# Half sums of 1024 elements, chunk scores in pairs, and q of the first two batches in rows of six tokens

## The chip, the cores and the metric

One core of one Trainium2 chip runs the whole program in one launch. The metric is the time of one execution on the device in microseconds (us), as the median of several runs. The core has TensorE (PE in the profile, PEld for its weight loads), VectorE (DVE), ScalarE (ACT), GpSimd (POOL) and SyncE (SP), which issues most of the DMA transfers.

## The reference

The first part is a retention layer written as a recurrence over 768 tokens, for 4 batches, 8 heads and 64 dimensions a head. The second part takes its output as x (768 tokens, 512 channels), adds a low-rank mixing of the tokens, and runs a two-layer MLP with 2048 hidden units.

```python
for t in range(S):
    state = gamma[None, :, None, None] * state + np.einsum('bhd,bhe->bhde', k[:, :, t], v[:, :, t])
    y[:, :, t] = scale * np.einsum('bhd,bhde->bhe', q[:, :, t], state)
...
x = np.ascontiguousarray(attn_out.transpose(0, 2, 1, 3)).reshape(B, S, H * D)
xt = x.transpose(0, 2, 1)
h = xt @ U @ V
u = x + h.transpose(0, 2, 1)
ch = np.maximum(u @ w_ch1, 0.0) @ w_ch2
return (u + ch).astype(np.float32)
```

U is 768 x 32, V is 32 x 768, w_ch1 is 512 x 2048, w_ch2 is 2048 x 512. All inputs and the output are 32-bit floats.

## The kernel before

The recurrence is computed in blocks: inside a block as a masked product of scores and v, between blocks through a state. Decay factors are multiplied into q, k and v beforehand. Everything that TensorE reads is bf16.

**The attention of batches 0 and 1** is worked by pairs of heads (`pair`, c = 0 to 3). One load per pair brings 2 heads of k, q or v (`load_pair`, 384 KB): a piece of the load is two tokens of one head, 512 bytes, and 768 pieces make the load. The rows are converted to bf16 (`kb`, `qb`, `vb`), TensorE turns k and q with a unit matrix (`turn`, L528), ScalarE copies the turned k to `kT`, and VectorE multiplies the turned q with a table of factors `gqt` and writes `qT` in the order of tokens (L544). Then come scores (64 of the array's rows each), a masked copy `a` (L567), the states `ns`, and `mix`, which gives two blocks of x.

**The attention of batches 2 and 3** is worked by chunks of 128 tokens and all 8 heads (`loads_chunk`, `chunk`, n = 0 to 5). Here the DMA queue of SyncE turns k and q (rows `kT<-kb`, `qT<-qb`). The scores of a chunk are 8 matmuls on 64 rows each into the two banks RR0, RR1; VectorE masks them in one operation of 1024 elements (L700); `mixes` adds state and block products in RR2; the result is copied to x.

**The mixing**: `proj` computes x with U in two steps, for tokens 0 to 511 and 512 to 767 (each matmul on 32 columns of the array), `expand` the product with V on 32 rows, which VectorE adds to x (L770), and u is turned for the MLP.

**The MLP** (`mlp`): for each of 16 blocks of hidden units, matmuls of uT with w1b for 512 tokens (part 0), then for the other 256 tokens (part 1), each followed by a ReLU to `gT`. The second layer is computed in the manner of Strassen and Winograd, with seven products in place of eight for each 256 tokens (r = 0, 1, 2). It needs sums and differences of halves of gT (`S1`, `S2`, `S4`, and one in the place of a quarter of gT) and of w2 (`T2`, `T3`, `T4`, and one in place). `sums` makes those of gT with four VectorE operations of 512 elements a call, four calls for part 0 and two for part 1 in each batch; `w2_sums` makes those of w2 once, four calls of four operations. The products of each r go to the banks M0, M1 and M2 in turn (`prod`), and are gathered by ScalarE (`s1`), GpSimd (`t12`, `t22`, `t21`: rows `t<-s,x`) and VectorE (`r5`, `r6`, and the outputs `oa`, `ob`: rows `r` and `o`). GpSimd's queue stores the outputs; for the last batch SyncE's does.

**What sets the order.** Nothing is scheduled by the compiler. Each step is handed to `Plan.add` with its cost by engine, the names that it reads and writes, and a wished time. `Plan.run` walks through the steps with these costs, takes at each point the step that can start first (by wished time among equals), and so fixes for each engine the order in which its instructions stand. On the chip every engine works through its own queue in that order and waits by semaphores for what it needs. The planner also has a model of the DMA queues (`Queues`; a load is priced by pieces, each 0.009 us and its size over 27,200 a us). Where TensorE would be free in the first 27 us, `fill` puts in matmuls of zeros (rows `M<-gT`). A VectorE sum that reads two tiles and a GpSimd operation planned behind it are tied in this order by `behind`. The weights are loaded by GpSimd's queue, which converts them to bf16 (`load_cast`); the loads of batch 1 wait by `gate`, a copy of one element on GpSimd, for the second, third and fourth block of w2.

Of the kernel before, what the change touches and what calls it, by code (L numbers as in the profile page):

```python
# [18 lines left out]
class Step:  # L19
# [181 lines left out]
def kernel(  # L201
# [12 lines left out]
    P = 128  # L214
# [249 lines left out]
    def load_pair(nm, b, c, at, hold=0.0, after=None, halves=False):  # L464

        t, key = new_in()
# [3 lines left out]
        src = {"k": k, "q": q, "v": v}[nm][b, ds(2 * c, 2)]  # L470
        for g in ([(0,), (1,)] if halves else [(0, 1)]):
# [4 lines left out]
                 P * n, 512, [(key, i) for i in g], at + 0.01 * g[0], hold,  # L476
# [3 lines left out]
    def pair(b, c, at, first, atq=0.0, atv=0.0):  # L480
# [47 lines left out]
        def turn(dst, src):  # L528
            def f(e):
                for b0 in range(NB):  # L530
                    for j in range(2):
                        tp(dst[:, ts(2 * b0 + j, P)], src[:, ds(384 * j + P * b0, P)])
            return f
        add({"PE": 0.34}, turn(Yb, kb), both2(kbk) + ["ident"], ["Y"], at + 0.6, F,
            slack=sl)
# [4 lines left out]
        add({"PE": 0.34}, turn(tq, qb), both2(qbk) + ["ident"], [tqk], atq + 0.9, F,  # L540
            slack=sl)
        qTv = qT.rearrange("x (b p j) -> x b j p", b=NB, j=2)
        tqv = tq[:, :S].rearrange("x (b j p) -> x b j p", b=NB, j=2)
        add({"D": 1.03}, lambda e: nc.vector.tensor_tensor(  # L544
            qTv, tqv, gqt[:, c].rearrange("x (b p j) -> x b j p", b=NB, j=2),
            op=ALU.mult), [tqk, ("gqt", c)], [qTk], atq + 1.2)
# [115 lines left out]
    def chunk(b, n, at):  # L662
        (kin, kk), (qin, qk), (vin, vk) = (gets.pop((nm, b, n)) for nm in "kqv")
# [33 lines left out]
        add({"PE": 0.24}, score, [kTk, qTk], ["RR0", "RR1"], at, ("rw", "rw"),  # L697
            slack=sl)
# [3 lines left out]
            RR[0].rearrange("p i (n t) -> p (i n) t", t=P),  # L702
            mask[:, None, :].to_broadcast([P, H, P]), op=ALU.mult),
            ["RR0", "RR1", "mask"], zz(ak), at + 0.3)
# [8 lines left out]
        def mixes(e):  # L713
            if n:
                prev = ns[:, ds(4 * ((n - 1) % 5), 4)]
                for c in range(NC):
                    mm(RR[1][:, 0, ts(c, P)], qT[:, ts(c, P)], prev[:, c], start=(c == 0))
            for c in range(NC):
                for i in range(2):
                    h = 2 * c + i  # L720
                    mm(RR[1][:, 0, ts(h, D)], av[:, i, c], vd[:, ts(h, D)],
# [3 lines left out]
        if n < NCK - 1:  # L725
# [7 lines left out]
            [qTk, *nsk, *zz(ak), *zz(vdk)], ["RR2"], at + 1.9, F, slack=sl)  # L733
        evac(xs[b % 2][:, n], RR[1][:, 0], DM, ["RR2"], xk(b, [n], ALLC), at + 2.4)


    def proj(b, at):
        sl = 0.3

        def f(js):  # L740
# [6 lines left out]
        add({"PE": 0.25}, f(range(4)), xk(b, range(4), ALLC) + ["Ub"], ["Y"], at,  # L747
            ("cn", "cn"), slack=sl)
        add({"PE": 0.13}, f(range(4, 6)), xk(b, range(4, 6), ALLC) + ["Ub"], ["Y"],
            at + 0.1, ("cn", "cn"), slack=sl)  # L750
        evac(pcs, Y[:, :P], P, ["Y"], ["pcs"], at + 0.3)

    def expand(b, j0, nj, at):
# [9 lines left out]
        for j in range(j0, j0 + nj, 2):  # L763
            for z in range(2):
# [7 lines left out]
                    kk + [("u", b % 2, i, z) for i in (j, j + 1)], at + 0.3)  # L772
# [41 lines left out]
    def next_m():  # L814
        mring[0] += 1
        return f"M{(mring[0] - 1) % 3}"

    def mlp(b, T, span, banks=()):
# [26 lines left out]
        for m in range(NM):  # L845
# [21 lines left out]
            relu(gT[:, m, :LO], bank, [bank], [("g", m, 0)], at + 0.9)  # L867
        yield
        for m in range(0, NM, 2):
# [13 lines left out]
            relu(gT[:, ds(m, 2), LO:], bank, [bank], [("g", m, 1), ("g", m + 1, 1)],  # L883
# [6 lines left out]
        def sums(part, m0, nm_, at):  # L890
# [5 lines left out]
            ek = [("g", 2 * m, part) for m in range(m0, m0 + nm_)]  # L896
            ok = [("g", 2 * m + 1, part) for m in range(m0, m0 + nm_)]
# [315 lines left out]
```

## Time and profile before

| | |
|---|---|
| median of 3 runs | 223.75 us (223.63 to 224.15) |
| profiled execution | 224.59 us, span 222.8 us |
| TensorE clock granted | 0.997 on the mean |
| instructions in the profile | 5876 |
| DMA | 35.22 MB in 85163 packets, mean 158 GB/s |
| VectorE, ScalarE, GpSimd busy | 65%, 50%, 39% of the span |

The times of the rows are those of the profiled execution. A row of a group gives the line of the code, the engine, the operation, what is written and read by the program's names, the shapes and the count, then busy time and the mean of one, then the idle time of the engine just before them and what ended it. The matmuls, copies and sums are recorded by helpers, so that many have the same line (L305 all matmuls, L302 all operations on two tiles); they are told apart by their names.

### The profile page before, as it was taken

Reading aid. Unit: us, or ns where it says so; the run is one execution under the profiler, and the core shown is the slowest. Engines: PE = TensorE matmul, PEld = TensorE weight load, DVE = VectorE, ACT = ScalarE, POOL = GpSimd, SP = SyncE. Lnnn points to the kernel's source line nnn. Section 1 sums busy time; section 2 is a strip of 40 time slices with the busy share of each in tenths; the row PEclk is TensorE's granted clock in tenths of the full one; section 3 lists DMA queues with packets and bytes.
Section 4 is the critical chain, followed back from the end, with each engine's and each line's share of the span. In section 5 each row is a group of like instructions: output and inputs, shape, how many; then the busy total and the mean of one; then the engine's idle time right before and its main releaser. Section 6 shows DMA issues by size and latency. Waiting matters only on the chain.

```text
span 222.8 us, 5876 instructions
## 1 busy us (share of the span) xinstructions
PE 211.8 (95%) x2391; PEld 152.4 (68%) x2405; DVE 143.9 (65%) x297; ACT 111.7 (50%) x214; POOL 87.0 (39%) x143
## 2 busy tenths in 40 slices
PE   7867999999999999999999999999999999999993
PEld 2556644488788885457887875458888854588882
DVE  4486717998897636798677856867858525345332
ACT  8856537679684335678621105686510036761000
POOL 4665900114768554311368453316134510003330
PEclk9999999999999999999999999999999999999998
DMA  5999999999599979897479989986105730000222
GB/s 167 301 291 224 157 195 206 233 289 297 140 222 212 154 205 182 218 170 142 96 158 190 222 195 202 195 187 123 26 0 143 181 106 3 0 0 3 94 97 94
DMA packets 85163, 35.22 MB, mean 158 GB/s; under 512 B 59920, under 2 KB 83216, under 8 KB 85136
## 3 DMA queue, kind: packets, MB, share of 16 engines
q1 hardware_dynamic: 78944, 25.93, 55.0%
q0 software_dynamic: 6192, 8.91, 19.3%
q8 instruction: 19, 0.31, 0.6%
q14 instruction: 8, 0.07, 0.1%
HBM read 27.75 MB, written 6.29 MB: 153 GB/s over the span
## 4 chain that ended last, share of the span: by engine, by line
PE 63%; DVE 16%; DMA 7%; POOL 5%; issue 4%; ACT 2%; SPq 1%; POOLq 0%; DVEq 0%
PE M L305 51%; PE RR L305 8%; DVE S L302 4%; DMA in<-in_v_dram 4%; DMA in<-in_k_dram 3%; PE Y L305 3%; DVE T L302 2%; POOL t L302 2%; DVE x L770 2%; ACT gT L836 1%; DVE gT L302 1%; SPq L342 1%; DVE o L945 1%; POOL out_dram L987 1%; DVE x L299 1%
## 5 line engine op out<-in xcount | busy, mean ns | idle before, releaser
L305 PE MATMUL M<-uT,w1b 128*128 128x256 bf16 (+1 forms) x489 | 85.7, 324 | 0.7 <-issue 0.3
L836 ACT ACTIVATE gT<-M 128x512 bf16<-128x512 f32 x88 | 51.9, 597 | 34.1 <-PE M L305 33.5
L305 PEld LDWEIGHTS <-w1b 128*128 128x128 bf16 x512 | 48.0, 98 | 29.6 <-issue 0.8
L305 PEld LDWEIGHTS <-gT 128*128 128x128 bf16 x409 | 39.3, 99 | 10.6 <-issue 3.7
L302 POOL TENSOR_TENSOR t<-s,x 128x256 f32<-128x256 f32 x36 | 23.1, 669 | 34.9 <-DVE S L302 21.8
L305 PEld LDWEIGHTS <-S 128*128 128x128 bf16 (+1 forms) x336 | 28.1, 97 | 4.4 <-issue 0.4
L305 PE MATMUL M<-w2b,gT 128*128 128x256 bf16 x192 | 26.7, 273 | 0.1
L305 PE MATMUL M<-w2b,S 128*128 128x256 bf16 x192 | 26.1, 273 | 0.3 <-DVE r L945 0.3
L305 PE MATMUL M<-T,gT 128*128 128x256 bf16 x192 | 25.1, 273 | 0.5 <-DVE r L945 0.4
L302 POOL TENSOR_TENSOR qb<-in,gqn 128x512 bf16<-128x512 f32 x12 | 12.5, 1044 | 27.9 <-DVE S L302 11.6
L302 DVE TENSOR_TENSOR S<-gT 128x512 bf16<-128x512 bf16 x24 | 11.6, 485 | 18.0 <-ACT gT L836 17.9
L945 DVE TENSOR_TENSOR r<-M,t 128x256 f32<-128x256 f32 x24 | 10.1, 421 | 12.6 <-POOL t L302 11.7
L297 ACT ACTIVATE s<-M 128x256 f32<-128x256 f32 x12 | 4.6, 385 | 26.7 <-PE M L305 26.7
L987 POOL DMA_DIRECT2D out_dram<-o x18 | 10.1, 563 | 19.3 <-DVE o L945 19.3
L770 DVE TENSOR_TENSOR x<-RR,x 128x512 bf16<-128x512 f32 x24 | 15.2, 683 | 2.1 <-PE RR L305 2.1
L297 ACT ACTIVATE kb<-in 128x512 bf16<-128x512 f32 (+1 forms) x18 | 10.0, 582 | 13.0 <-DMA in<-in_k_dram 12.9
L700 DVE TENSOR_TENSOR a<-RR,mask 128x1024 bf16<-128x1024 f32 x12 | 14.6, 1218 | 1.4 <-PE RR L305 1.2
L302 POOL TENSOR_TENSOR vb<-in,gkn 128x512 bf16<-128x512 f32 x12 | 12.5, 1045 | 6.8 <-DMA in<-in_v_dram 3.0
L945 DVE TENSOR_TENSOR o<-M,r 128x256 f32<-128x256 f32 x24 | 10.1, 423 | 6.4 <-PE M L305 6.1
L305 PE MATMUL M<-T,S 128*128 128x256 bf16 x96 | 12.6, 273 | 0.0
L297 ACT ACTIVATE ns<-Y 64x256 bf16<-64x256 f32 (+1 forms) x24 | 9.4, 392 | 5.4 <-PE Y L305 3.8
L302 DVE TENSOR_TENSOR gT<-gT 128x512 bf16<-128x512 bf16 x24 | 11.5, 481 | 0.6
(104 smaller groups left out, 258.4 us busy)
## 6 DMA issues: line engine op xcount, KB each, us to landing
out_dram<-o POOLq DMA_DIRECT2D x18, 256.0 KB, 3.5
in<-in_q_dram SPq DMA_DIRECT2D x8, 384.0 KB, 6.0
in<-in_k_dram SPq DMA_DIRECT2D x12, 256.0 KB, 5.0
in<-in_q_dram SPq DMA_DIRECT2D x12, 256.0 KB, 4.5
in<-in_v_dram SPq DMA_DIRECT2D x12, 256.0 KB, 4.7
in<-in_k_dram SPq DMA_DIRECT2D x7, 384.0 KB, 6.2
in<-in_v_dram SPq DMA_DIRECT2D x7, 384.0 KB, 6.3
w2b<-in_moe_w_ch_dram POOLq DMA_DIRECT2D x4, 512.0 KB, 15.2
```

What stands on the lines that cost most here:

```text
L297: nc.scalar.activation(dst, src, AF.Copy)
L299: (nc.vector if e == "D" else nc.gpsimd).tensor_copy(out=dst, in_=src)
L302: (nc.vector if e == "D" else nc.gpsimd).tensor_tensor(dst, a, b, op=op)
L305: nc.tensor.matmul(out_, lhsT, rhs, start=start, stop=stop, skip_group_check=True)
L342: nc.sync.dma_start(out=dst, in_=src)
L700: add({"D": cD(2 * DM)}, lambda e: nc.vector.tensor_tensor(a[:, :2 * DM].rearrange("p (n t) -> p n t", t=P), RR[0].rearrange("p i (n t) -> ...
L770: add({"D": cD(512)}, lambda e, xj=xj, src=src: nc.vector.tensor_tensor(xj, src, xj, op=ALU.add), [f"RR{c}" for c in cc] + kk, kk + [("u", ...
L836: nc.scalar.activation(dst, src, AF.Relu)
L945: add({"D": cD(HD)}, lambda e: nc.vector.tensor_tensor(dst, bankof(bank)[:, :HD], src, op=op), [bank] + rd, wr, at - 2)
L987: lambda e: (nc.sync if last else nc.gpsimd).dma_start(out=dst, in_=src), rd, [("out", b, at)], at,
```

## The change

It has these parts:

- **Half sums of 1024 elements.** `sums` is called for part 0 twice, with twice the blocks, and for part 1 once; this call is given inside the products of r = 0, and its first operation also waits for `t21`. `w2_sums` takes two blocks at a time. The difference that is written into gT has a name of its own (`h`), so that products which read only the untouched quarter don't wait for it.
- **Chunk scores in pairs.** `chunk` hands its scores to `chunks`, which puts those of two chunks into one step; the even chunk uses the banks RR0, RR1 for scores and mix, the odd one RR2, RR3.
- **proj in one step**, for all 768 tokens. The additions of `expand` have a later wished time from batch 2 on.
- **q of batches 0 and 1 in rows of six tokens.** A piece of such a load is six tokens of one head, 1536 bytes, 256 pieces a load. The casts keep the six tokens apart; TensorE turns six blocks; VectorE reads the turned q with steps of 128 elements and writes `qT` in order.
- **The planner** lets a VectorE step that needs the step just before it wait for its end (it was its release), prices the weight loads without the factor 1.17 and at half the fixed part, counts q loads as shorter, and keeps the loads of batch 0 in the order in which they are written.

The numbers of TensorE's matmuls, by kind, are the same but for the matmuls of zeros (17 where there were 20 of 512 columns into M, and none in place of 2 into Y).

```diff
-            t = max(t, p.free if p.eng == e else p.end + Plan.LAG[p.eng] + s.slack)
+            t = max(t, p.free if p.eng == e != "D" else
+                    p.end + (0.03 if p.eng == e else Plan.LAG[p.eng] + s.slack))
...
-            dma=(nd, 0.009 + size / 27200 * 1.17, 0.9, 1.0), hold=hold)
+            dma=(nd, 0.0045 + size / 27200, 0.9, 1.0), hold=hold)
...
+        first = [] if b else ["in"]
+        if nm == "q":
+            load(t.rearrange("p (i x) -> p i x", i=2),
+                 src.rearrange("i (p j) d -> p i (j d)", p=P), 256, 1536,
+                 [(key, i) for i in range(2)] + first, at, hold, late=0.2 - 0.2 * b)
+            return
...
-            cast(turned(qb, i), given(qin, i), 384, [(qk, i)], [(qbk, i)],
+            cast(qb.rearrange("p (j i d) -> p i j d", i=2, d=D)[:, i],
+                 qin[:, ts(i, 384)].rearrange("p (j d) -> p j d", d=D), 384,
+                 [(qk, i)], [(qbk, i)],
                  atq + 0.1 * i, eng="AP" if first else "A")
...
-        qTv = qT.rearrange("x (b p j) -> x b j p", b=NB, j=2)
-        tqv = tq[:, :S].rearrange("x (b j p) -> x b j p", b=NB, j=2)
+        tqv = tq[:, :S].rearrange("x (j p) -> x p j", j=NCK)
         add({"D": 1.03}, lambda e: nc.vector.tensor_tensor(
-            qTv, tqv, gqt[:, c].rearrange("x (b p j) -> x b j p", b=NB, j=2),
-            op=ALU.mult), [tqk, ("gqt", c)], [qTk], atq + 1.2)
+            qT.rearrange("x (p j) -> x p j", j=NCK), tqv,
+            gqt[:, c].rearrange("x (p j) -> x p j", j=NCK), op=ALU.mult),
+            [tqk, ("gqt", c)], [qTk], atq + 1.2)
...
+        z = n % 2
+        keys = [f"RR{2 * z}", f"RR{2 * z + 1}"]
+
         def score(e):
             for c in range(NC):
                 for i in range(2):
                     r = ds(64 * i, 64)
-                    mm(RR[0][:, i, ts(c, P)], kT[r, ts(c, P)], qT[r, ts(c, P)])
-        add({"PE": 0.24}, score, [kTk, qTk], ["RR0", "RR1"], at, ("rw", "rw"),
-            slack=sl)
+                    mm(RR[z][:, i, ts(c, P)], kT[r, ts(c, P)], qT[r, ts(c, P)])
+        yield score, [kTk, qTk], keys
...
+    def chunks(b, n, at):
+        two = [chunk(b, n + z, at + DN * z) for z in range(2)]
+        told = [next(c) for c in two]
+
+        def scores(e):
+            for f, _, _ in told:
+                f(e)
+        add({"PE": 0.45}, scores, [k_ for t_ in told for k_ in t_[1]],
+            [k_ for t_ in told for k_ in t_[2]], at + DN, ("rw", "rw"), slack=0.4)
+        for c in two:
+            list(c)
...
-        add({"PE": 0.25}, f(range(4)), xk(b, range(4), ALLC) + ["Ub"], ["Y"], at,
+        add({"PE": 0.37}, f(ALLN), xk(b, ALLN, ALLC) + ["Ub"], ["Y"], at,
             ("cn", "cn"), slack=sl)
-        add({"PE": 0.13}, f(range(4, 6)), xk(b, range(4, 6), ALLC) + ["Ub"], ["Y"],
-            at + 0.1, ("cn", "cn"), slack=sl)
...
-                    kk + [("u", b % 2, i, z) for i in (j, j + 1)], at + 0.3)
+                    kk + [("u", b % 2, i, z) for i in (j, j + 1)],
+                    at + (6.3 if b > 1 else 0.3))
...
-                (S1[:, ms, r], A(0, 1), A(1, 1), ALU.add, ek + ok, sk("S1")),
-                (A(0, 1), A(0, 0), A(0, 1), ALU.subtract, ek, ek),
+                (S1[:, ms, r], A(0, 1), A(1, 1), ALU.add,
+                 ek + hk + ok + ["t21"] * part, sk("S1")),
+                (A(0, 1), A(0, 0), A(0, 1), ALU.subtract, ek, hk),
...
-        for q4 in range(4):
-            sums(0, 2 * q4, 2, T + unit * (0.864 * 4 * (q4 + 1) + 1.0))
-        for q4 in range(2):
-            sums(1, 4 * q4, 4, T + unit * (13.8 + 0.872 * 4 * (q4 + 1) + 1.0))
+        for z in range(2):
+            sums(0, 4 * z, 4, T + unit * (0.864 * 8 * (z + 1) + 1.0))
...
+            if r == 0:
+                sums(1, 0, 8, at + 1)
...
-        for j in range(4):
-            ms = ds(2 * j, 2)
+        for j in range(0, 4, 2):
+            ms = ds(2 * j, 4)
+            wk, tk = [("w2", j), ("w2", j + 1)], [("T", j), ("T", j + 1)]
...
-                chunk(b, n, base + 2 + 4.6 * n)
+                if n % 2:
+                    chunks(b, n - 1, base + 2 + 4.6 * (n - 1))
```

More of the change, by code (lines that the diff above doesn't have):

```diff
@@ L475, in load_pair @@
                      "i (n p j) d -> p (i n) (j d)", p=P, j=2),
-                 P * n, 512, [(key, i) for i in g], at + 0.01 * g[0], hold,
+                 P * n, 512, [(key, i) for i in g] + first, at + 0.01 * g[0], hold,
                  late=0.0 if b else 0.7 if nm + str(c) in ("v1", "v2", "v3") else 0.2,
@@ L524, in pair, with turn @@
         for i in range(2):
-            cast(turned(qb, i), given(qin, i), 384, [(qk, i)], [(qbk, i)],
+            cast(qb.rearrange("p (j i d) -> p i j d", i=2, d=D)[:, i],
+                 qin[:, ts(i, 384)].rearrange("p (j d) -> p j d", d=D), 384,
+                 [(qk, i)], [(qbk, i)],
                  atq + 0.1 * i, eng="AP" if first else "A")
-        def turn(dst, src):
+        def turn(dst, src, at_):
             def f(e):
-                for b0 in range(NB):
-                    for j in range(2):
-                        tp(dst[:, ts(2 * b0 + j, P)], src[:, ds(384 * j + P * b0, P)])
-            return f
-        add({"PE": 0.34}, turn(Yb, kb), both2(kbk) + ["ident"], ["Y"], at + 0.6, F,
-            slack=sl)
+                for j in range(NCK):
+                    tp(dst[:, ts(j, P)], src[:, ds(at_(j), P)])
+            return f
+        add({"PE": 0.34}, turn(Yb, kb, lambda j: 384 * (j % 2) + P * (j // 2)),
+            both2(kbk) + ["ident"], ["Y"], at + 0.6, F, slack=sl)
         evac(kT, Yb[:, :S], S, ["Y"], [kTk], at + 0.7, eng="A")
@@ L716, in mixes @@
                 for c in range(NC):
-                    mm(RR[1][:, 0, ts(c, P)], qT[:, ts(c, P)], prev[:, c], start=(c == 0))
+                    mm(RR[z][:, 0, ts(c, P)], qT[:, ts(c, P)], prev[:, c], start=(c == 0))
             for c in range(NC):
@@ L866, in mlp @@
                         [bank], at + 0.4 * z, F)
-            relu(gT[:, m, :LO], bank, [bank], [("g", m, 0)], at + 0.9)
+            relu(gT[:, m, :LO], bank, [bank], [("g", m, 0), ("h", m, 0)], at + 0.9)
         yield
@@ L896, in sums @@
             ek = [("g", 2 * m, part) for m in range(m0, m0 + nm_)]
+            hk = [("h", 2 * m, part) for m in range(m0, m0 + nm_)]
             ok = [("g", 2 * m + 1, part) for m in range(m0, m0 + nm_)]
@@ L924, in mlp @@
             ek = [("g", m, part) for m in range(0, NM, 2)]
+            hk = [("h", m, part) for m in range(0, NM, 2)]
             ok = [("g", m, part) for m in range(1, NM, 2)]
```

29 lines of the change are left out of this document (15 added, 14 removed).

## The prediction

> **What bounds the kernel now.** I read the page first, then the stages, then what TensorE waits for. A row of the stages reads: stretch, its length, then the busy time of PE, PEld, DVE, ACT and POOL with instruction counts, granted clock, DMA share, GB/s.
>
> ```profile
> PE 211.8 (95%) x2391; PEld 152.4 (68%) x2405; DVE 143.9 (65%) x297; ACT 111.7 (50%) x214; POOL 87.0 (39%) x143
> 0.00:10.00 10.00, 7.91 (x59) 3.91 (x60) 3.90 (x26) 8.81 (x12) 5.41 (x20) 1.00 0.83 228
> 10.00:20.00 10.00, 7.67 (x179) 5.78 (x180) 8.10 (x9) 5.55 (x10) 6.46 (x10) 1.00 1.13 273
> 150.00:160.00 10.00, 10.00 (x122) 8.61 (x120) 7.68 (x12) 7.22 (x14) 4.07 (x5) 1.00 0.47 92
> PE RR L305 <- DVE qT L544: 1.5, 2, 0.8
> PE M L305 <- DVE r L945: 0.6, 3, 0.3
> ```
>
> TensorE works for 95% of the span. Outside the first 20 us it is hardly ever idle: a stretch like 150 to 160 us is full, at the full granted clock (1.00). The list of its waits is short, 1.5 us for qT in the first batch and 0.6 us in three waits for `r`. So after the start TensorE's queue itself is the bound; what another engine saves counts only where TensorE waits for it, and what counts most is TensorE's own time and the time at which its dense part begins. The first 20 us are paced by loads (DMA share 1.13, TensorE busy 7.67 of 10 us, part of that with matmuls of zeros).
>
> A change that is measurable here is one over 0.2%, about 0.45 us. The profiled execution took 224.59 us, 222.8 of them span, and lies 0.84 above the median of 223.75. I sum the terms as differences against this execution and take them off the median.
>
> **Scores and projection joined: less TensorE time.** The change joins the scores of two chunks into one step (16 matmuls on 64 rows, where there were 8 and 8 with other work between), and the two steps of `proj` into one. In the instruction order, from the first chunk of batch 2 on, TensorE changes between tilings (full array, 64 rows, 32 rows, 32 columns) 42 times before and 26 times after: 6 score visits fewer and 2 projection visits fewer, two changes for each. Matmuls are the same in number. What a visit costs beyond its matmuls (start, length, what):
>
> ```profile
> 137.18 2.75 PE L305 MATMUL M<-uT,w1b 128*128 128x512 bf16 x12
> 139.86 0.40 PE L305 MATMUL RR<-qT,kT 64*128 64x128 bf16 x8
> 140.19 0.40 PE L305 MATMUL Y<-vb,kb 128*128 128x128 bf16 x4
> 140.42 2.32 PE L305 MATMUL M<-uT,w1b 128*128 128x512 bf16 x9
> 164.68 1.05 PE L305 MATMUL M<-T,gT 128*128 128x256 bf16 x8
> 165.66 0.30 PE L305 MATMUL Y<-x,Ub 128*32 128x128 bf16 x8
> 165.88 1.05 PE L305 MATMUL M<-w2b,S 128*128 128x256 bf16 x8
> 168.07 1.05 PE L305 MATMUL M<-T,S 128*128 128x256 bf16 x8
> 168.96 1.04 PE L305 MATMUL M<-w2b,S 128*128 128x256 bf16 x8
> ```
>
> Compare starts. Four full matmuls of 128 columns take 140.19 to 140.42, 0.23 us. Eight on half the rows run two at a time and should take the same, yet take 139.86 to 140.19, 0.33: 0.10 on leaving. On entering: eight of 256 columns take 164.68 to 165.66, 0.98, in front of the projection, and 168.07 to 168.96, 0.89, in front of a full step: 0.09. The projection's eight, four at a time, need 0.11 and take 0.22: again 0.11. So a visit costs 0.20 to 0.22, and 8 visits 1.6 to 1.8 us. TensorE is full there, so this lies on the path: **-1.7 us**. In the earlier batches 75 changes become 73; I count 0 for that.
>
> **Half sums of 1024 elements.** Per batch 24 VectorE operations of 512 become 12 of 1024, and 16 of w2 become 8.
>
> ```profile
> L770 DVE TENSOR_TENSOR x<-RR,x 128x512 bf16<-128x512 f32 x24 | 15.2, 683 | 2.1 <-PE RR L305 2.1
> L700 DVE TENSOR_TENSOR a<-RR,mask 128x1024 bf16<-128x1024 f32 x12 | 14.6, 1218 | 1.4 <-PE RR L305 1.2
> L302 DVE TENSOR_TENSOR S<-gT,S 128x512 bf16<-128x512 bf16 x24 | 10.2, 424 | 0.7
> 203.22 1.92 POOL L302 TENSOR_TENSOR t<-s,x 128x256 f32<-128x256 f32 x3 [21.81 <-DVE S L302]
> 203.92 0.42 DVE L945 TENSOR_TENSOR r<-M,t 128x256 f32<-128x256 f32 x1 [0.85 <-POOL t L302]
> 204.40 1.03 PE L305 MATMUL M<-T,gT 128*128 128x256 bf16 x8 [0.18 <-DVE r L945]
> ```
>
> 512 more elements cost 535 ns from PSUM (1218 less 683). An all-bf16 sum is shorter by 259 at the same size (683 against 424), so I take it to run at half that per element: 424 + 267, some 0.69 us in place of two times 0.42. That is 0.16 saved for each of 56 pairs, 9 us of VectorE's 143.9. It is beside full TensorE work and worth nothing by itself. What is on the path is the order: the sums of the last 256 tokens move from ahead of GpSimd's `t` to behind it. In the last three rows `t` waits for a sum, `r` for `t`, and TensorE 0.18 us for `r`; the three waits of that kind (0.6 us in all) should go. In exchange four sums of 0.69 now stand among the `r` and `o` of the first 256 tokens. There a bank must be read within one product of 0.87 us, and 0.42 + 0.69 is 1.11, so up to 0.24 can come back per sum; I take 0.3 in all, as most land in gaps. Net **-0.3 us**, with bounds of -0.6 and +1.0. The join of two chunk masks (2 x 1.218 us one behind the other) is in the same upper bound; the `r` and `o` queued behind a pair wait longest, and two of the six pairs stand among products.
>
> **q in rows of six tokens: the start.** A q load of batches 0 and 1 becomes 256 pieces of 1536 bytes where there were 768 of 512.
>
> ```profile
> 8.00:16.00 8.00, 5.49 (x112) 3.68 (x114) 6.53 (x7) 5.24 (x10) 5.92 (x10) 1.00 1.17 290
> 24.00:42.00 18.00, 17.37 (x178) 8.63 (x173) 10.81 (x24) 9.99 (x22) 4.48 (x10) 1.00 1.19 192
> 20.09 0.52 ACT L297 ACTIVATE vb<-in 128x384 bf16<-128x384 f32 x1 [1.74 <-DMA in<-in_v_dram]
> 20.67 0.83 PE L305 MATMUL M<-vb,kb 128*64 128x256 bf16 x20 [0.72 <-ACT vb L297]
> 27.94 0.59 PE L305 MATMUL M<-uT,w1b 128*128 128x512 bf16 x2 [0.16 <-issue]
> ```
>
> At 290 GB/s a load of 393 KB takes 1.36 us, which is 28 ns for a piece of 512 bytes on each of 16 engines. The kernel's own price for a load (0.009 us and the size over 27,200 a us) gives the same 28, and 65 ns for 1536 bytes: 1.05 us a load. Lower bound of the saving: nothing, if bytes and not pieces set the 290. Upper bound: the weight loads that convert move 192 GB/s into the chip, so read twice that, 384; at this rate a load takes 1.02, 0.34 less. I take 0.31, near the upper end, as the kernel's price meets the one measured point. Four q loads stand ahead of the last v, so it can land 1.24 us earlier. The path does run through it: ScalarE waits 1.74 us for v and TensorE 0.72 for ScalarE. But the last v loads also share the engines with U, V and the first weights, so I take **-0.9 us**, from 0 to -1.3. The matmuls of zeros fill what TensorE has free before 27 us and cost nothing.
>
> [...]
>
> **q's turn on VectorE.** The multiplication reads the turned q in PSUM with steps of 256 bytes and writes in order; it read in order and wrote with steps of 4 bytes.
>
> ```profile
> L544 DVE TENSOR_TENSOR qT<-RR,gqt 128x768 bf16<-128x768 bf16 x4 | 4.1, 1028 | 2.6 <-PE RR L309 2.6
> L544 DVE TENSOR_TENSOR qT<-M,gqt 128x768 bf16<-128x768 bf16 x4 | 4.1, 1020 | 2.8 <-ACT kT L297 2.4 <-PE M L309 0.5
> 45.00:58.00 13.00, 12.83 (x157) 11.27 (x156) 10.92 (x25) 10.40 (x22) 5.33 (x12) 1.00 1.08 288
> ```
>
> 1.02 us for 768 elements with steps in the output and in gqt is the same slope as 1218 for 1024: those steps cost nothing. Whether steps in PSUM do, no row shows. I take 0, as both other stepped operands are free; a gain has no reason, since 1.04 ns an element is already the pace without steps. The other end is the third rival. The casts of q keep their element count.
>
> **Order of batch 1: loads that come just in time.** In the new order batch 1's first k is converted after one ReLU of the last 256 tokens, not after five, and turned by TensorE after 32 matmuls of 256 columns, not after 64. Eight of these take 0.87, so both come 3.5 us earlier, and 0.9 more by the earlier start.
>
> ```profile
> L342 SPq DMA_DIRECT2D in<-in_k_dram x1: 384/384/384, 40.4 to 40.4; - x1
> DMA to landing us min/median/max: 6.2/6.2/6.2
> 49.88 0.93 ACT L297 ACTIVATE kb<-in 128x384 bf16<-128x384 f32 x2
> 51.80 0.50 PE L309 MATMUL Y<-ident,kb 128*128 128x128 bf16 x6
> ```
>
> That load was issued at 40.4 and landed at 46.6; its conversion ran at 49.9. It is now wanted at 45.5, so ScalarE would wait 1.1 us, with the next ReLUs queued behind it. The load's issue waits for the second block of w2, and the weight stream sets that: it is no shorter in bytes, and its second load now stands behind the conversion of U in GpSimd's queue, though U is asked for ahead of V. TensorE arrives at its turn at 47.4 and the conversion ends at 47.5, so there it hardly waits, but the ReLU queued behind ends near 48.1, and TensorE wants that bank some 0.4 earlier. Later q loads are 0.3 shorter each, so it does not build up. I take **+0.5 us**, from 0 to +2.
>
> **The sum.** -1.7 - 0.3 - 0.9 + 0.5 = -2.4 us: the span goes from 222.8 to about 220.4, the median from 223.75 to 221.35, or **221.4**. Its own range is 219.9 to 222.6.
>
> **Rivals.**
> First, batch 1's loads decide. If each conversion of k and q waits 1.1 us or more and TensorE, which takes its queue in order, inherits two such waits, the term is +2.0 in place of +0.5: 222.9. For: wanted at 45.5, landed at 46.6. Against: three M banks between TensorE and ScalarE.
>
> Second, the start doesn't move: the q loads take as long as before, or the tail of v is set by what it shares the engines with. Then 221.35 + 0.9 = 222.3. For: 393 KB remain 393 KB. Against: 290 GB/s with small pieces where the weight stream reads 384.
>
> Third, on the other side: the stepped read in PSUM goes at half the pace. Then 768 elements cost 0.8 us more, eight times. Of the four in batch 0, VectorE has 1.47 us free in 8 us (6.53 busy), which hides half of the 3.2: +1.2 with the wait of TensorE for qT (1.5 us now) growing. Of the four in batch 1, in a stretch where VectorE has 2.1 free in 13 us and full queues after it, half comes out: +1.6. That gives 224.2; with the waits for the loads on top 224.4, slower. It decides from about 0.7 us a multiplication. [...]
>
> Fourth, a larger gain: the waits of batch 1 vanish with the reordering (the loads' +0.5 is 0 and the start is at its upper end): 220.1 or less.
>
> **Chances.** Forecast 0.50; first rival 0.17; second 0.14; third 0.11; fourth 0.08. All but the third and a tail of the first are below 223.3. So faster by over 0.2% 0.80, within it 0.08, slower 0.12. For eight in ten the range goes from 219.6 to 223.7; it leaves out the third rival and the end of the fourth.
>
> **What would show it.** In the profile after: TensorE's score rows of 16 with one 0.2 us visit per pair, and `x,Ub` rows of 24 with nothing between; VectorE sums of 1024 at about 690 ns; `qT` still at 1.02 us (near 1.8, the third rival holds); the last v conversion of batch 0 near 19.2 instead of 20.1, and the first matmul of uT with w1b near 27.0 instead of 27.9; batch 1's first k conversion waiting for its load by about 1 us; no wait of TensorE for `r` behind `t`. The prediction is wrong if TensorE's idle time after 30 us grows by more than 2 us, or if its busy time after 60 us does not shrink by 1.5.

## The result and the profile after

The changed kernel takes 222.0 us (median of 4 runs, 221.89 to 222.32) where the kernel before takes 223.69 beside it (4 runs, 223.25 to 224.15). The ratio is 0.992, with a 95% interval of 0.990 to 0.994. The profiled execution took 222.32 us with a span of 220.6, against 224.59 and 222.8 before: 2.2 us less span.

The page's line of busy times of the kernel after, and then its stages, with the columns of the prediction's first fence:

```profile
PE 210.2 (95%) x2388; PEld 151.8 (69%) x2400; DVE 133.8 (61%) x245; ACT 112.1 (51%) x210; POOL 89.9 (41%) x143
```

```profile
8.00:16.00 8.00, 5.18 (x104) 3.54 (x102) 6.33 (x7) 5.92 (x11) 6.15 (x9) 1.00 1.13 320
45.00:58.00 13.00, 11.61 (x151) 9.38 (x151) 9.67 (x15) 10.28 (x24) 8.32 (x13) 1.00 1.03 299
150.00:160.00 10.00, 10.00 (x121) 9.01 (x116) 5.51 (x8) 4.84 (x10) 4.82 (x6) 1.00 0.52 105
```

VectorE is busy 10 us less, TensorE 1.6. From 8 to 16 us the transfers move 320 GB/s where they moved 290. From 45 to 58 us TensorE works 11.61 of 13 us where it worked 12.83: a hole of 1.2 us that was not there. TensorE's waits (total, times, longest), and the rows in order of time around that hole (start, length, what, and in brackets the idle time before and what ended it):

```profile
PE Y L310 <- ACT kb L298: 1.2, 1, 1.2
PE RR L306 <- DVE qT L552: 0.7, 1, 0.7
```

```profile
41.16 0.39 SPq L343 DMA_DIRECT2D in<-in_k_dram  x1
47.39 0.94 ACT L298 ACTIVATE kb<-in 128x384 bf16<-128x384 f32 x2 [2.23 <-DMA in<-in_k_dram]
48.38 0.51 PE L310 MATMUL Y<-ident,kb 128*128 128x128 bf16 x6 [1.24 <-ACT kb L298]
51.36 1.50 PE L306 MATMUL M<-uT,w1b 128*128 128x256 bf16 x12 [0.15 <-ACT gT L861]
```

Rows of the same view from the start, from a joined pair of chunks in batch 2, and from the last batch:

```profile
17.72 0.51 POOL L300 CAST vb<-in 128x384 bf16<-128x384 f32 x1 [0.79 <-DMA in<-in_v_dram]
19.15 0.83 PE L306 MATMUL M<-vb,kb 128*64 128x256 bf16 x20
19.54 0.52 ACT L298 ACTIVATE vb<-in 128x384 bf16<-128x384 f32 x1
20.98 1.04 PE L306 MATMUL M<-vb,kb 128*64 128x256 bf16 x20
25.25 1.31 PE L306 MATMUL RR<-uT,w1b 128*128 128x512 bf16 x3
27.16 0.59 PE L306 MATMUL M<-uT,w1b 128*128 128x512 bf16 x2
...
133.79 1.89 PE L306 MATMUL M<-uT,w1b 128*128 128x512 bf16 x8
135.61 0.62 PE L306 MATMUL RR<-qT,kT 64*128 64x128 bf16 x16
136.16 0.40 PE L306 MATMUL Y<-vb,kb 128*128 128x128 bf16 x4
...
201.49 0.42 DVE L972 TENSOR_TENSOR r<-M,t 128x256 f32<-128x256 f32 x1 [0.20 <-POOL t L303]
201.59 1.04 PE L306 MATMUL M<-T,gT 128*128 128x256 bf16 x8
```

The groups of VectorE that the change touches:

```profile
L303 DVE TENSOR_TENSOR S<-gT,S 128x1024 bf16<-128x1024 bf16 x12 | 8.3, 693 | 0.1
L552 DVE TENSOR_TENSOR qT<-RR,gqt 128x768 bf16<-128x768 bf16 x4 | 3.8, 954 | 1.4 <-PE RR L310 1.3
L552 DVE TENSOR_TENSOR qT<-M,gqt 128x768 bf16<-128x768 bf16 x4 | 3.8, 950 | 2.2 <-PE M L310 2.2
```

And of the kernel before, the product of the last v with `kb`:

```profile
22.34 0.83 PE L305 MATMUL M<-vb,kb 128*64 128x256 bf16 x20
```

The score rows are of 16 matmuls now. Batch 0 has four loads of v, and the product of each with `kb` is 20 matmuls. The third load is the one whose conversion waited at 20.09 before; its conversion now starts at 17.72, and its product at 19.15 instead of 20.67. The last one's conversion starts at 19.54 (20.84 before), and its product at 20.98 instead of 22.34. The first k of batch 1 is issued at 41.16 (40.40 before) and its conversion, 2.23 us idle, starts at 47.39; TensorE waits 1.24 us for it and finds the next bank late again at 51.36. In the last batch no wait of TensorE for `r` is left.

To compare executions I read three points off the matmul rows of each trace: **A**, the start of batch 0's first up product of 256 columns; **B**, the start of its last product of `w2b` with `gT`, close to the end of the down products; **C**, the start of the last matmul. The start ends at A, batch 1's loads arrive between A and B, and the chunks lie between B and C.

| kernel | A | A to B | B to C | C |
|---|---|---|---|---|
| before | 44.81 | 37.46 | 136.86 | 219.13 |
| after | 43.49 | 38.56 | 134.81 | 216.86 |
| after minus before | -1.32 | +1.10 | -2.05 | -2.27 |

### The profile page after: what moved, and what is told of

Read it like the earlier page. It is cut to its first block, busy times and chain, and to the rows that moved or that the text cites. A ratio compares the mean times of both kernels' runs of the same rounds, so it can differ in the third digit from the quotient of the medians.

```text
span 220.6 us, 5820 instructions
## 1 busy us (share of the span) xinstructions
PE 210.2 (95%) x2388; PEld 151.8 (69%) x2400; DVE 133.8 (61%) x245; ACT 112.1 (51%) x210; POOL 89.9 (41%) x143
## 4 chain that ended last, share of the span: by engine, by line
PE 74%; DMA 16%; POOL 3%; SPq 2%; ACT 2%; issue 1%; DVE 0%; ACTq 0%; DVEq 0%
PE M L306 63%; PE RR L306 7%; DMA w2b<-in_moe_w_ch_dram 7%; DMA in<-in_v_dram 6%; PE Y L306 3%; DMA in<-in_k_dram 3%; SPq L343 2%; POOL w1b L353 1%; POOL vb L300 1%; PE RR L310 1%; PE Y L310 1%; ACT gT L861 0%; ACT kb L298 0%; DVE o L972 0%; ACT qb L298 0%
## 5 line engine op out<-in xcount | busy, mean ns | idle before, releaser
L306 PE MATMUL M<-w2b,S 128*128 128x256 bf16 x192 | 26.7, 273 | 0.0
L1016 POOL DMA_DIRECT2D out_dram<-o x18 | 10.2, 566 | 17.4 <-DVE o L972 17.4
L712 DVE TENSOR_TENSOR a<-RR,mask 128x1024 bf16<-128x1024 f32 x12 | 14.1, 1218 | 4.8 <-PE RR L306 4.8
L303 DVE TENSOR_TENSOR S<-gT 128x1024 bf16<-128x1024 bf16 x12 | 8.4, 697 | 13.0 <-ACT gT L861 12.7
L298 ACT ACTIVATE kb<-in 128x512 bf16<-128x512 f32 (+1 forms) x17 | 9.4, 577 | 10.8 <-DMA in<-in_k_dram 10.8
L298 ACT ACTIVATE x<-RR 128x512 bf16<-128x512 f32 (+2 forms) x17 | 10.2, 609 | 8.1 <-PE RR L306 7.9
L576 DVE TENSOR_TENSOR a<-RR,mask 128x1024 bf16<-128x1024 f32 (+1 forms) x12 | 11.0, 951 | 3.7 <-PE RR L306 3.7
```

What stands on the lines that cost most here:

```text
L298: nc.scalar.activation(dst, src, AF.Copy)
L303: (nc.vector if e == "D" else nc.gpsimd).tensor_tensor(dst, a, b, op=op)
L306: nc.tensor.matmul(out_, lhsT, rhs, start=start, stop=stop, skip_group_check=True)
L576: lambda e, bs=bs, lo=lo, w=w: nc.vector.tensor_tensor(av[:, :, ds(bs[0], len(bs))], RR[lo // 2][:, :, :w].rearrange("p i (b t) -> p i b t ...
L712: add({"D": cD(2 * DM)}, lambda e: nc.vector.tensor_tensor(a[:, :2 * DM].rearrange("p (n t) -> p n t", t=P), RR[z].rearrange("p i (n t) -> ...
L1016: lambda e: (nc.sync if last else nc.gpsimd).dma_start(out=dst, in_=src), rd, [("out", b, at)], at,
```

## The experiments

**Theory 1**, formed from these points: joined visits save what the prediction said; the start gains 1.3 us by the q rows; most of that is lost again between A and B, as TensorE comes to batch 1's first k before the load has landed; VectorE's shorter sums are hidden. **Rival a**: what is late is the load itself, as GpSimd's queue issues the weights later. **Rival b**: the shorter sums are the gain. **Rival c**: time saved at the start is paid back later whatever is done. All kernels below are edits of the changed kernel. The chips of these runs read 224.0 to 224.4 us for the kernel before, and single times scatter more (six runs of one kernel: 220.8 to 223.5), so ratios carry intervals of about 0.004, and the traces carry the argument. Two of the traces hold a stretch of 3.4 us at half the granted clock, worth up to 1.7 us: a2_after ahead of A, e10_halved between A and B; e12_wsteps holds one of 17.1 us ahead of A.

| kernel | us | ratio to before, 95% | A | A to B | B to C |
|---|---|---|---|---|---|
| e1_price | 220.73 | 0.983 (0.979 to 0.987) | 43.41 | 36.58 | 135.80 |
| e2_unpair | 223.03 | 0.993 (0.990 to 0.997) | 42.78 | 37.66 | 135.82 |
| e3_qrows | 222.44 | 0.992 (0.989 to 0.995) | 44.95 | 37.13 | 134.30 |
| e6_w1early | 221.23 | 0.985 (0.981 to 0.989) | 43.36 | 36.88 | 134.83 |
| a2_after | 221.87 | 0.988 (0.984 to 0.992) | 44.08 | 38.20 | 134.84 |
| e6b_w1early | 220.81 | 0.983 (0.979 to 0.988) | 44.14 | 37.55 | 134.81 |
| e8_w1early_unpair | 222.14 | 0.989 (0.984 to 0.994) | 43.73 | 37.75 | 135.82 |
| e9_w1early_sums512 | 224.04 | 0.997 (0.994 to 1.000) | 42.98 | 39.05 | 135.33 |
| e10_halved | 222.96 | 0.994 (0.991 to 0.997) | 43.37 | 41.30 | 135.31 |
| e11_proj2 | 220.96 | 0.985 (0.981 to 0.989) | 43.11 | 36.90 | 134.91 |
| e12_wsteps | 233.55 | 1.040 (1.037 to 1.044) | 51.94 | 40.86 | 135.01 |
| e7_both | 220.44 | 0.983 (0.979 to 0.987) | 43.45 | 36.58 | 135.01 |

**The turn 32 matmuls later: e1_price.**

```diff
-            dma=(nd, 0.0045 + size / 27200, 0.9, 1.0), hold=hold)
+            dma=(nd, 0.009 + size / 27200 * 1.17, 0.9, 1.0), hold=hold)
```

> The changed kernel with the old price for a weight load in the planner (0.009 + size/27200 x 1.17), nothing else. In this order TensorE turns batch 1's first k block after 64 quarter-up matmuls instead of 32, some 3.5 us later, as in the kernel before. Theory 1 (the wait of 1.24 us for batch 1's first k and the gaps around it, about 1.7 us together, cost the end because TensorE comes to the turn before the load has landed): the PE wait for kb at 46 to 51 us falls under 0.4 us and the time comes to 220.9 us (220.3 to 221.4). Rival c (the start's gain is paid back later whatever is waited for there): 222.0 us, with idle time of PE after 52 us larger by over 1 us.

TensorE's queue at the turn, with nothing idle ahead of it:

```profile
43.74 6.82 PE L306 MATMUL M<-uT,w1b 128*128 128x256 bf16 x61
50.40 0.60 PE L306 MATMUL M<-w2b,gT 128*128 128x256 bf16 x4
50.84 0.50 PE L310 MATMUL Y<-ident,kb 128*128 128x128 bf16 x6
```

A to B is 2.0 us shorter than in the changed kernel, and the time 220.73: theory 1 as expected. One microsecond of it was given back between B and C (135.80), where rival c put it, but 0.6 of that is a wait for one turned q, by DMA, and e7_both, with the same TensorE order, has 135.01. So what came back here was one late transfer, and no rule as rival c has it.

**Weights issued earlier: e6_w1early, twice, beside a2_after.**

```diff
-                  hold=(18.0, 19.5, 21.5, 24.0, 26.5)[i])
+                  hold=(18.0, 18.1, 21.5, 24.0, 26.5)[i])
```

> The changed kernel with the second w1 load held until 18.1 instead of 19.5 in the planner's time, so that GpSimd's queue issues it right behind the first, ahead of the last v cast and of Ub; the last v cast goes from GpSimd to ScalarE. The orders of TensorE, VectorE and the sync queue are the same. Rival a (batch 1's first k is late because the weight loads ahead of it were issued 0.8 us later, behind the casts of GpSimd): the second w1 load issues by 20.7 us, the gate of the w2 block and with it batch 1's first k about 0.8 us earlier, the PE wait of 1.24 us falls under 0.5 us, and the time to 221.2 us (220.8 to 221.6). Theory 1 in its narrow form (only TensorE's order matters, the load's place is set by the bytes ahead of it): k lands within 0.3 us of where it landed, 222.0 us (221.7 to 222.3).

> The changed kernel itself, to stand on the same chip as the three below. 222.0 us on a chip where the kernel before takes 223.7; its ratio again 0.990 to 0.994. Theory 1: k of batch 1 is waited for again, between 0.3 and 1.3 us, as its landing comes from transfers and differs by up to 1.6 us between executions of one order (ScalarE's first cast of it started at 47.39 us here, at 45.8 and 46.1 us in two kernels with the same or nearly the same order of issues).

> The kernel with the second w1 load issued ahead of the last v cast, on the same chip as the changed kernel. If its gain is real and comes from batch 1's first k: 0.8 to 1.2 us under the changed kernel beside it, with no PE wait for that k over 0.3 us. If it was the luck of one chip: within 0.4 us of the changed kernel.

GpSimd's queue, first of the changed kernel, then of e6_w1early (start, length, what):

```profile
20.68 0.50 POOL L300 CAST vb<-in 128x384 bf16<-128x384 f32 x1 [1.58 <-DMA in<-in_v_dram]
21.42 2.50 POOL L353 DMA_DIRECT2D w1b<-in_moe_w_ch_dram  x3
40.83 0.55 POOL L462 CAST in<-w2b 1x1 f32<-1x1 bf16 x3 [12.85 <-DMA w2b<-in_moe_w_ch_dram]
```

```profile
18.34 1.68 POOL L353 DMA_DIRECT2D w1b<-in_moe_w_ch_dram  x2
21.06 1.49 POOL L353 DMA_DIRECT2D w1b<-in_moe_w_ch_dram  x2
39.03 0.42 POOL L462 CAST in<-w2b 1x1 f32<-1x1 bf16 x3 [12.42 <-DMA w2b<-in_moe_w_ch_dram]
45.58 0.94 ACT L298 ACTIVATE kb<-in 128x384 bf16<-128x384 f32 x2 [0.56 <-DMA in<-in_k_dram]
```

In the changed kernel the second w1 load stands behind the last conversion of v, which waits 1.58 us for its data, and behind that of U. Issued ahead of them, the weights free the gate of batch 1's k earlier, by 1.8 us (39.03 against 40.83) and by 1.3 in the pair on one chip (39.81 against 41.09), TensorE's wait for k goes from 1.24 and 0.88 us to none and 0.24, A to B is 0.65 us shorter at the least, and the time beside the changed kernel is 1.06 us lower (220.81 against 221.87). Rival a holds: the place of the weight issues in GpSimd's queue set the landing. The narrow form of theory 1 falls; the two are one wait seen from its two ends, and either end removes it. With both removed (e7_both) nothing more is won:

> The old price for a weight load in the planner and the second w1 load early, together. Theory 1: TensorE's order is that of the kernel with the old price, which waited for no k of batch 1, so an earlier load has nothing left to remove: 220.4 to 220.9 us where the kernel before takes 224.3, a ratio of 0.982 to 0.985. If the loads of batch 1 set the time in any other way, lower than 220.2 us.

220.44 us, as theory 1 said. With e1_price and e6_w1early it lies 1.5 to 1.7% under the kernel before, where the changed kernel lies 0.8 and 1.2% under it; the three can't be told apart.

**Scores one chunk at a time: e2_unpair, and e8_w1early_unpair on e6_w1early.**

```diff
-        add({"PE": 0.45}, scores, [k_ for t_ in told for k_ in t_[1]],
-            [k_ for t_ in told for k_ in t_[2]], at + DN, ("rw", "rw"), slack=0.4)
+        for z, (f, rd, wr) in enumerate(told):
+            add({"PE": 0.24}, f, rd, wr, at + DN * z, ("rw", "rw"), slack=0.4)
```

> The changed kernel with the two chunks' score products as two steps that the planner places one by one, as before the change; the projections stay in one step, half sums stay at 1024 elements, q stays in rows of six tokens. Theory 1 (a visit of TensorE to another tiling costs 0.20 to 0.22 us, and the change joins eight of them): six visits come back, +1.3 us, 223.3 us (222.8 to 223.8), and the idle time of PE after 60 us grows by about that much while its busy time hardly moves. Rival b (the gain of the chunk phase comes from VectorE's shorter sums): no change, 222.0 us (221.7 to 222.3).

> The kernel above with the chunks' score products as two steps again, so that the wait for batch 1's k stays out of the comparison. Theory 1 (six visits at 0.20 to 0.22 us come back): +1.0 to +1.5 us on the kernel above, between the end of batch 0's down products and the end of those of batch 2, where a trace shows it free of the start. Rival b (shorter VectorE is what gained): within 0.3 us of it.

Score rows of e2_unpair:

```profile
132.68 0.40 PE L306 MATMUL RR<-qT,kT 64*128 64x128 bf16 x8
133.01 0.40 PE L306 MATMUL Y<-vb,kb 128*128 128x128 bf16 x4
```

B to C is 135.82 in both, 1.01 more than 134.81: 12 changes of tiling come back (38 where there were 26), 0.084 us each, 0.17 a visit and not 0.20 to 0.22. The planner moved steps of the other queues too, but in e2_unpair TensorE is busy for all of the 135.82 us (in e6_w1early for 134.73 of 134.83), so the extra is its own time; the expectation had looked for it in idle time. On one chip e8_w1early_unpair stands 1.33 us above e6b_w1early. The time of e2_unpair alone would not tell: its ratio of 0.993 is near the changed kernel's 0.992 and 0.988, as its TensorE did not meet the wait for k. Rival b's "no change" falls for this part.

**proj in two steps: e11_proj2, on e6_w1early.**

```diff
-        add({"PE": 0.37}, f(ALLN), xk(b, ALLN, ALLC) + ["Ub"], ["Y"], at,
+        add({"PE": 0.25}, f(range(4)), xk(b, range(4), ALLC) + ["Ub"], ["Y"], at,
             ("cn", "cn"), slack=sl)
+        add({"PE": 0.13}, f(range(4, 6)), xk(b, range(4, 6), ALLC) + ["Ub"], ["Y"],
+            at + 0.1, ("cn", "cn"), slack=sl)
```

> The kernel with the second w1 load early, with each projection x,Ub as two steps again (4 + 2 of the 6 chunks); pairs, sums and q rows stay. Theory 1 (two visits to the tiling of 32 columns come back): 0.3 to 0.5 us more between the end of batch 0's down products and the last matmul, 135.1 to 135.3 us; the time +0.4 us on the kernel it is based on. Rival b: 134.8 us there.

134.91, only 0.10 more: the expectation was wrong. In this order the two steps stand mostly one behind the other, and the count of tiling changes goes from 26 to 27, not to 30. One change for 0.10 us fits the price, though e7_both, without it, has 135.01. The kernel before had four more changes for `proj`, and this run brings back one of them, so it does not measure what joining `proj` brought; by 0.084 us a change, an estimate from e2_unpair, the four are 0.34.

**q in rows of two tokens: e3_qrows.**

```diff
-        if nm == "q":
-            load(t.rearrange("p (i x) -> p i x", i=2),
-                 src.rearrange("i (p j) d -> p i (j d)", p=P), 256, 1536,
-                 [(key, i) for i in range(2)] + first, at, hold, late=0.2 - 0.2 * b)
-            return
...
-            qT.rearrange("x (p j) -> x p j", j=NCK), tqv,
-            gqt[:, c].rearrange("x (p j) -> x p j", j=NCK), op=ALU.mult),
+            qTv, tqv, gqt[:, c].rearrange("x (b p j) -> x b j p", b=NB, j=2),
+            op=ALU.mult),
...
-        t += 1.07 if n[0] == "q" else 1.36
+        t += 1.36
```

> The changed kernel with q of batches 0 and 1 loaded as before the change, in rows of two tokens (512 bytes), cast and turned in the old order, the multiplication out of PSUM reading in order and writing with steps, and the loads paced as before. Theory 1 (the start gained 1.3 us by the rows, the load of batch 1's k lost about the same): the first product with the up weights of 256 columns starts 1.2 us later (44.7 us instead of 43.5), qT takes 1.02 us again instead of 0.95; what batch 1's first k costs is smaller as TensorE comes later, so the time is between 222.3 and 223.4 us, 222.8 likeliest. Rival (rows do nothing, the start's gain comes from the order of the steps): first up product at 43.5 us and 222.0 us.

A is at 44.95, as before the change (44.81); with the long rows it lies between 42.78 and 44.14 in eleven traces, 43.4 on the mean. From 8 to 16 us the transfers move 291 GB/s again, and the third v waits until 19.96. So the rows, with the planner's pace of loads that belongs to them, are worth some 1.5 us at A; it is one trace, and the eleven differ by 1.4. At C little of it is left: e3_qrows starts its last matmul at 216.38, the changed kernel at 216.86 and 217.12, as the later start meets batch 1's k on time. It takes 0.992 of the kernel before, where the changed kernel took 0.992 and 0.988. Without the wait the rows do reach the end (e6_w1early: 215.07 and 216.50).

**Sums of 512: e9_w1early_sums512, then e10_halved.** The first plans and issues them as before the change, on e6_w1early; the second keeps the plan of 1024 and issues each sum in two halves, so that every queue has e6_w1early's order.

```diff
-        for z in range(2):
-            sums(0, 4 * z, 4, T + unit * (0.864 * 8 * (z + 1) + 1.0))
+        for q4 in range(4):
+            sums(0, 2 * q4, 2, T + unit * (0.864 * 4 * (q4 + 1) + 1.0))
...
-                sums(1, 0, 8, at + 1)
+                sums(1, 0, 4, at + 1)
+                sums(1, 4, 4, at + 1.4)
...
-        for j in range(0, 4, 2):
-            ms = ds(2 * j, 4)
+        for j in range(4):
+            ms = ds(2 * j, 2)
...
```

> The kernel with the second w1 load early, with half sums of 512 elements as before the change (pairs and q rows stay). Theory 1: VectorE is busy 8 to 10 us longer, but its idle time hides nearly all of it: 0 to +0.5 us. Rival b: +1.0 us or more.

```diff
-                    both(e, dst, a_, b_, op), rd, wr, at, lock="D")
+                    halves(e, dst, a_, b_, op), rd, wr, at, lock="D")
...
+    def halves(e, dst, a, b, op):
+        n = dst.shape[1] // 2
+        for z in range(2):
+            both(e, dst[:, ds(n * z, n)], a[:, ds(n * z, n)],
+                 b[:, ds(n * z, n)], op)
```

> The kernel with the second w1 load early; the planner still plans half sums of 1024 elements, so that all five queues stand in the same order, but each sum is issued as two instructions of 512 one behind the other. From the kernel with sums of 512, two back to back take 0.75 us where one of 1024 takes 0.68: 56 sums x 0.07 us = VectorE busy 4 us longer. Theory 1 (VectorE's time is hidden, and what the sums of 512 cost in the other kernel came from the order planned with them): from the end of batch 0's down products to the last matmul 134.8 to 135.1 us (134.8 with sums of 1024), the time within 0.4 us of the kernel with the second w1 load early. Rival b: +1 us or more.

Both cost more than theory 1 allowed: 224.04 beside 220.81 on one chip, and a ratio of 0.994 where e6_w1early had 0.985 and 0.983. B to C grows by 0.5 us in both, for e10_halved 0.2 more than was expected (135.31 against 135.1). The rest is between A and B. The trace of e10_halved is of an execution of 225.58 us, and 1.7 of its 41.30 between A and B go to the half clock; e9_w1early_sums512 has no such stretch. GpSimd's gates there, rows in order of time, of e6_w1early and then of e10_halved with what followed, and two stages of e10_halved:

```profile
44.61 2.05 POOL L462 CAST in<-w2b 1x1 f32<-1x1 bf16 x4 [1.81 <-DMA w2b<-in_moe_w_ch_dram]
```

```profile
45.15 4.92 POOL L468 CAST in<-w2b 1x1 f32<-1x1 bf16 x5 [1.93 <-DMA w2b<-in_moe_w_ch_dram]
48.80 0.75 DVE L303 TENSOR_TENSOR T<-w2b,T 128x512 bf16<-128x512 bf16 x2
49.47 0.95 DVE L558 TENSOR_TENSOR qT<-RR,gqt 128x768 bf16<-128x768 bf16 x1
49.74 0.37 SPq L349 DMA_DIRECT2D in<-in_q_dram  x1
59.11 0.94 ACT L298 ACTIVATE kb<-in 128x384 bf16<-128x384 f32 x2 [2.08 <-DMA in<-in_k_dram]
62.04 0.42 PE L312 MATMUL RR<-qT,kT 64*64 64x128 bf16 x16 [1.75 <-ACT kT L298]
```

```profile
60.00:62.00 2.00, 0.30 (x3) 0.02 (x1) 0.65 (x2) 1.98 (x5) 1.59 (x2) 1.00 1.16 294
62.00:66.00 4.00, 3.96 (x56) 2.85 (x57) 2.30 (x3) 1.68 (x4) 2.24 (x4) 0.58 0.99 198
```

The gates are copies of one element. The first of these five ran from 45.15 for 4.44 us, to the very end of VectorE's unbroken row of bf16 sums of 512 (qT follows at 49.47); the other four took 0.17 each. The next load of SyncE, the sixth of batch 1, went out at 49.74; it went at 45.49 and 47.37 in the two profiles of e6_w1early, where four copies beside VectorE's sums of 1024 took 2.05 and 2.44 us (one took 0.66 us at the median in the changed kernel's trace). So q and k of batch 1 come late a second time: ScalarE waits 2.08 us for a k, TensorE 1.75 for ScalarE. e9_w1early_sums512 has the same copy, 4.59 us from 43.85, and a wait of 1.5 us at 60.0. Before the change VectorE's sums in that stretch start 0.34 to 0.46 us apart, 0.42 long each, and the copies take 0.17 to 0.40 us.

The 0.66 us for a copy is about the length of one sum beside it (0.68 us); the 4.44 us reach over a dozen instructions one behind the other. What holds the copy up, no run shows. So rival b is right in part: VectorE's time is hidden, but not the order in which GpSimd gets through, and that gates the loads.

**Steps written instead of steps read: e12_wsteps** (on e6_w1early, all queues in the same order).

```diff
-        tqv = tq[:, :S].rearrange("x (j p) -> x p j", j=NCK)
+        tqv = tq[:, :S].rearrange("x (j p) -> x j p", j=NCK)
...
-            qT.rearrange("x (p j) -> x p j", j=NCK), tqv,
-            gqt[:, c].rearrange("x (p j) -> x p j", j=NCK), op=ALU.mult),
+            qT.rearrange("x (p j) -> x j p", j=NCK), tqv,
+            gqt[:, c].rearrange("x (p j) -> x j p", j=NCK), op=ALU.mult),
```

> The kernel with the second w1 load early, where the multiplication of the turned q reads PSUM in order and writes SBUF with steps of six elements, as the changed kernel's twin; all queues stand in the same order. Theory 1 (VectorE's read of PSUM in steps costs nothing, the write in steps cost 0.07 us of 1.02): qT takes 1.00 to 1.05 us instead of 0.95, and the time stays within 0.3 us, as only the last step of the start waits for qT. Rival (steps are free on either side and the old time came from the two groups of 384 that the old form had): 0.95 us.

Neither: 233.55 us, 4% above the kernel before. The groups, the waits and two stages of the start:

```profile
L552 DVE TENSOR_TENSOR qT<-RR,gqt 128x768 bf16<-128x768 bf16 x4 | 11.0, 2751 | 1.5 <-PE RR L310 1.5
L552 DVE TENSOR_TENSOR qT<-M,gqt 128x768 bf16<-128x768 bf16 x4 | 10.9, 2734 | 1.6 <-PE M L310 1.6
```

```profile
PE RR L306 <- DVE qT L552: 10.2, 7, 2.6
```

```profile
15.00:20.00 5.00, 3.11 (x56) 2.37 (x56) 4.48 (x4) 2.29 (x5) 3.72 (x7) 0.59 1.11 248
20.00:25.00 5.00, 4.33 (x88) 3.51 (x91) 4.26 (x4) 1.60 (x4) 5.00 (x9) 0.50 1.30 174
```

A multiplication takes 2.74 us where the changed kernel's takes 0.95. TensorE waits 10.2 us in all, and after waits of 2.5 and 2.6 us it also works at half the clock (0.59 granted from 15 to 20 us, 0.50 from 20 to 25). With steps of two elements (before, and e3_qrows) it took 1.02. Whether the step of 12 bytes in the output or that of 24 bytes in `gqt`, 32-bit, costs this was not separated.

## Why the prediction came out right, step by step

221.4 was predicted and 222.0 measured; the span fell by 2.2 us where the sum said 2.4, the median by 1.7. The terms behind it were less right than their sum. By the three points the start gained 1.32 us for 0.9, the loads lost 1.10 for 0.5, and the chunks gained 2.05 for the 2.0 of joined visits and half sums. That the first two errors cancel is luck.

- **Joined visits, -1.7.** The kind of cost was right and its size too high: 1.0 for the scores (e2_unpair, e8_w1early_unpair), and by the same price 0.34 for `proj`, an estimate, as e11_proj2 undid a quarter of it. The step that failed is the subtraction of neighbouring starts for one visit; 0.084 us a change is what twelve changes together show.
- **Half sums, -0.3 with bounds of -0.6 and +1.0.** The size of one was right (0.69 us forecast, 683 to 732 ns by kind), and the waits for `r` behind `t` went. In the chunks the sums are worth 0.5 (e10_halved). "Worth nothing by itself" failed between A and B: in the new order sums of 512 would have cost 1.5 us or more there, as GpSimd's gates came through late (one copy took 4.44 us in e10_halved, 4.59 in e9_w1early_sums512). The 1.0 of the scores and the 0.5 of the sums are 1.5 of the 2.05 gained between B and C; with the estimate for `proj` it is 1.8, and no run separates the rest.
- **The start, -0.9.** Right in kind and too small: 1.3 between the two traces, 1.5 by e3_qrows. The 290 GB/s became 320, and 291 in e3_qrows, so pieces and not bytes alone had set it, and the second rival falls. The price of a load was right: in the traces the second to fourth q land 1.06 to 1.09 us after the load ahead of them, where it was 1.36. The path was right too, but the step misread its row: the conversion at 20.09, with the waits of 1.74 and 0.72 us behind it, is that of the third v and not of the last. It starts 2.4 us earlier, though the fourth q landed only 0.64 earlier; why the third v gained so much more, no run separates. The products of the last two v start 1.5 and 1.4 us earlier, close to the gain at A. The first product of uT with w1b came 0.8 us earlier (27.16) in M, and others of its kind, into RR, stand ahead of it from 25.25.
- **Batch 1's loads, +0.5.** The place was right, the size was not: +1.1 between A and B, with 1.24 us of TensorE's own wait where "hardly waits" was forecast. The step that failed is the arrival: the load was taken at 46.6 as before, with TensorE at its turn at 47.4; TensorE was there at 47.1, and the conversion started at 47.39. The load was issued 0.76 us later, since the second w1 load stood behind v and U in GpSimd's queue, which the step had named and then passed over, and TensorE came earlier by the larger start. The first rival's other condition, two inherited waits, did not come.
- **q's turn, 0.** 0.95 us for 1.02, a gain of 0.07 where the text saw no reason for one. Its own rows had the reason: 683 ns for 512 elements and 1218 for 1024 put 768 without steps at 950, so 1020 was not the same slope. The third rival's price (0.7 us a multiplication) is excluded for the read; the half pace that it supposed was shown by no run, and the stepped read took 0.95 us. But "those steps cost nothing", said of the written side and of `gqt`, holds, but for the 0.07 us, for steps of two elements; with six the old direction would have cost more than the rival asked (2.74 us in e12_wsteps).

TensorE's busy time after 60 us shrank by 1.7, from 158.2 to 156.5, and its idle time after 30 us grew by 0.4, from 5.3 to 5.7, so both of the prediction's own conditions held.

## What to carry to other kernels

When a start is made faster, follow every transfer that the later stage needs back to the queue that issues it: what waits there, behind a conversion for another reader, can give the gain back (here 1.10 of 1.32 us). Price a mode change or a fixed cost over many of them, undone together, rather than from one pair of rows. And when steps in memory can stand on the read or the written side, measure both (here 0.95 and 2.74 us).

## What the runs showed that was not expected

- VectorE's read of PSUM in steps of 128 bf16 elements costs nothing (0.95 us for 768, the slope of 683 for 512 and 1218 for 1024); steps of six elements in the output and the 32-bit table cost 1.8 us more (2.74 us, e12_wsteps).
- Beside VectorE's bf16 sums of 512 in an unbroken row a one-element copy on GpSimd took 4.4 us (e10_halved); beside sums of 1024 one took 0.66.
- After a wait of TensorE of 1.75 us the granted clock fell to half for 3.4 us (e10_halved), after those of 2.5 and 2.6 us for 17.1, five times as long (e12_wsteps); both are worked out from the granted clocks of the stages. The length of the wait alone does not decide: in a2_after the clock fell for 3.4 us, from about 16.5, after a wait of 1.2 us, while the changed kernel's first trace, with the same wait of 1.20 us and the later one of 1.24, and e9_w1early_sums512, with 1.5 us at 60.0, kept the full clock. What makes the clock fall in one execution and not in the next stays open. Such a wait can cost more than its own length: 3.4 us at half clock are up to 1.7 us of lost work.
